# Retention and mixture of experts on one core: tile loads in two halves of 64 partitions, the second one paced by TensorE

## The chip, the core and the metric

The kernel runs on one core of a Trainium2 chip. The metric is the device time of one execution in microseconds, the median of several runs. The profile is that of one further execution. All data are float32; matrix products are done in float32 in the first stage and, in the second, as three products of a high and a low part in a reduced format (a value is split into what the format holds and the rest).

## What is computed

```python
# q, k, v: (8, 8, 576, 64)     retention, causal, with a decay per head
scores = scale * np.matmul(q, k.transpose(0, 1, 3, 2))
ret = scores * Dmat[None, :, :, :]          # Dmat = gamma_h ** (i - j) for j <= i, else 0
attn = np.matmul(ret, v)
x = attn.transpose(0, 2, 1, 3).reshape(4608, 512)

# mixture of 8 experts, top 1
e_idx = np.argmax(x @ w_gate, axis=1)
gate_w = softmax(x @ w_gate)[np.arange(N), e_idx]
eom = 1.0 / (1.0 + np.exp(-(x @ w_output_gate)))
for e in range(8):
    h = np.maximum(x[mask] @ w1[e], 0.0)    # w1: (8, 512, 1024)
    out[mask] = gate_w[mask, None] * eom[mask, e, None] * (h @ w2[e])   # w2: (8, 1024, 512)
```

## The kernel before

There are two stages. The retention stage walks over 36 tiles of 128 tokens (`NTILE`), 9 to two batches, in one loop over `g` (lines 573 to 631). The expert stage then takes the tokens of each expert, at most 616 slots (`CAP`), and multiplies them with the expert's two weight matrices (`mm1`, `mm2`, lines 247 to 290).

A tile's q, k and v lie in DRAM as one block, `pack[g]`: 128 partitions by 3 x 512 numbers, 768 KB. `load(g)` (line 306) takes a buffer from a pool of five (`ld`, `LD = 5`) and issues one DMA on SP's queue. In tile `g` of the loop, `load(g + 4)` is called; the buffer that it gets is the one of tile `g - 1`, whose last reader is `by_state(g - 1)` on TensorE.

The engines keep the order of the program (`manual_schedule`, line 570). In tile `g` that order is, as far as it matters here:

- SP: `load_k(g + 1)` (line 336: for odd tiles from 3 to 31 that don't end a batch pair, k by rows, 256 KB, into one of two buffers that `update` frees), `load(g + 4)`, then by `weights(g)` (line 554) perhaps a block of 512 KB of expert 0's weights. In tile 31 also the first gathered rows and their indices (`load_rows`, `load_idx`), which wait for the scatters issued up to tile 30.
- POOL: `prep(g + 1)` (line 352), which multiplies the tile's v by a decay, giving `vp`; later one or two scatters of finished tokens into the experts' slots (line 629).
- TensorE: `scores(g + 1)` (line 357, q times k, with products on the rows 0 to 63 and 64 to 127 apart), `by_state(g)` (line 399, q times the state), `outT(g)` (line 412: S V, 8 products of the masked scores with `vp`, added to what `by_state` left in PSUM), `update(g)` (line 383, the state), `k_rows(g + 1)` (line 342, k transposed, in the tiles where it isn't loaded), `xnat(g - 1)` (line 525, the finished tile transposed and the gate's logits).
- ACT copies the state (line 396), k and the finished tile out of PSUM; DVE masks the scores (line 378), scales the tile's output (line 422) and works out the gate for four tiles at a time.

Expert 0's weights come in eight blocks in the same loop. `wsched` gives for each the tile of its DMA, of its cast on ACT (`hi_w`) and of its subtraction on DVE (`lo_w`). The table `pe` holds one TensorE instruction; `read(paced=True)` in the expert stage makes a DMA wait for it.

Of the kernel before, what the change touches and what calls it, by code (L numbers as in the profile page):

```python
# [10 lines left out]
F32 = mybir.dt.float32  # L11
# [8 lines left out]
SYNC = mybir.DependencyInfo(mybir.DependencyClass.Sync, mybir.DependencyReason.DATA)  # L20
# [6 lines left out]
P = 128  # L27
NP = H // 2
NTILE = NT // P
# [4 lines left out]
TA = -(-CA // P)  # L34
SNAP = 5
# [5 lines left out]
GT = 4  # L41
# [7 lines left out]
def tile_retention_moe(  # L49
# [16 lines left out]
    V, A, G, T, SP = nc.vector, nc.scalar, nc.gpsimd, nc.tensor, nc.sync  # L66
# [58 lines left out]
    const.tile([P, 16], F32, name="shift0")  # L125
    W1, W2 = {}, {}

    def start_w(which, e, fp):
        src, shape = (w1, [P, KB, 256]) if which == 1 else (w2, [P, 2, DM])
        st = wst.tile(shape, F32, name="st")  # L130
        SP.dma_start(out=st, in_=src[e, fp].rearrange("p (a b) -> p a b", a=shape[1]))
        if which == 2 and not W2:
            wpool.tile([P, 48], F32, name="shift1")
        hi = wpool.tile(shape, F32R, name=f"w{which}h{fp}")
        lo = wpool.tile(shape, F32R, name=f"w{which}l{fp}")
        (W1 if which == 1 else W2)[e, fp] = (hi, lo)
        return st, hi, lo

    def hi_w(st, hi, lo):
        for h in range(2):  # L140
            k = slice(h * st.shape[1] // 2, (h + 1) * st.shape[1] // 2)
            A.copy(out=hi[:, k], in_=st[:, k])  # L142
# [14 lines left out]
    pe = [None]  # L157
# [3 lines left out]
    def read(paced=False, first=None, **kw):  # L161
        i = SP.dma_start(**kw)
        if paced:
            tc.add_manual_dep(i.ins, pe[0].name, SYNC, reason="not before TensorE is at this point")
        for j in scat if first is None else first:
            tc.add_manual_dep(i.ins, j.name, SYNC, reason="reads the rows after every scatter so far")
        tc.add_to_no_dep_group("xs", i.ins)

    def load_rows(e, t, first=None):
        XG[e, t] = xg.tile([P, DM], F32, name="x_g")  # L170
        o, m = e * NT + ROW0[t], ROWS[t]
        read(first=first, out=XG[e, t][0:m], in_=xs[o:o + m, 0:DM])
# [9 lines left out]
    def load_idx(e, part, first=None):  # L182
        ts = range(TA) if part == 0 else range(TA, CT)
        if e == 0 and part == 0:
            for t in ts:
                o, m = ROW0[t], ROWS[t]
                read(first=first, out=idx[0:m, e, t], in_=xs[o:o + m, DM:DM + 2].bitcast(I32))
        else:
            o = e * NT + ROW0[ts[0]]
            read(out=idx[:, e, ts[0]:ts[-1] + 1],  # L190
                 in_=xs[o:o + P * len(ts), DM:DM + 2].rearrange("(t p) w -> p t w", p=P).bitcast(I32))
# [29 lines left out]
    def transp(e, t):  # L221
        transp_lo(*transp_hi(e, t))
# [71 lines left out]
    ld = actx.enter_context(tc.tile_pool(name="ld", bufs=LD, side="right"))  # L294
# [5 lines left out]
    pk, kn, vs, xT, gt = {}, {}, {}, {}, {}  # L300
# [2 lines left out]
    sc = ps_s.tile([P, 2, 512], F32, name="sc")  # L303
    o_ps = ps_s.tile([P, 2, 512], F32, name="o_ps")

    def load(g):
        t = ld.tile([P, 3, 512], F32, name="pk")
        SP.dma_start(out=t, in_=pack[g])
        pk[g] = t

    def load_first():
        t = [ld.tile([P, 3, 512], F32, name="pk") for _ in range(4)]
# [23 lines left out]
    def load_k(g):  # L336

        if g < NTILE and g % CPB != 8 and by_rows(g):
            kn[g] = wk.tile([P, DM], F32, name="kn")
            SP.dma_start(out=kn[g], in_=krow[g])  # L340
# [42 lines left out]
    def update(g):  # L383

        c = g % CPB
        if c == 8:
            return
        if c in (0, 4):
            st_ps[0] = ps_1.tile([P, NP, D], F32, name="st_ps")
        lo = 64 if c == 4 else 0  # L390
        for p in range(NP):
            for r in range(2):
                o = P * p + 64 * r
                T.matmul(st_ps[0][64 * r:64 * r + 64, p, :], lhsT=kn[g][lo:P, o:o + D], rhs=vs[g][lo:P, 2 * p + r, :],  # L394
                         start=(c in (0, 4) and p == 0), stop=True, skip_group_check=True)
        A.copy(out=stT[g % 2], in_=st_ps[0])
        stcur[0] = stT[g % 2]
# [14 lines left out]
    def outT(g, S_sb, state):  # L412
        o = o_ps
        c = g % CPB
        part = lambda p, r: o[64 * ((p + r) % 2):64 * ((p + r) % 2) + 64, r, P * (p // 2):P * (p // 2) + P]

        for r, p in ((r, p) for r in range(2) for p in range(NP)):
            T.matmul(part(p, r), lhsT=vs[g][:, 2 * p + r, :], rhs=S_sb[:, r, p, :],
                     start=(state is None and p < 2), stop=True, skip_group_check=True)
        x = wk.tile([P, NP, P], F32, name="xT")  # L420
        c0 = P * c if c < 5 else 64 + P * (c - 5)
        V.tensor_tensor(out=x.rearrange("p (r s) i -> p r s i", r=2),
                        in0=o[:, :, 0:2 * P].rearrange("p r (s i) -> p r s i", s=2),
                        in1=gq_sb[:, :, c0:c0 + P].rearrange("p (r s) i -> p r s i", r=2), op=ALU.mult)
        xT[g] = x
# [120 lines left out]
    for r in range(2):  # L546
        T.matmul(sc[:, r], lhsT=zx[:, 0:P], rhs=zx[:, 0:512], start=True, stop=True)
    prep(0)

    wsched = {(1, 0): (4, 7, 7), (1, 1): (7, 11, 11), (1, 2): (11, 15, 15), (1, 3): (15, 19, 19),  # L550
              (2, 0): (19, 23, 23), (2, 1): (23, 27, 27), (2, 2): (27, 31, 31), (2, 3): (34, 36, 36)}
    wparts = {}

    def weights(g):
        for w, at in wsched.items():
            if g == at[0]:
                wparts[w] = start_w(w[0], 0, w[1])
            if g == at[1]:
                hi_w(*wparts[w])

    def weights_lo(g, part=range(2)):
        for w, at in wsched.items():
# [7 lines left out]
    with tc.manual_schedule():  # L570
        S_next = scores(0)
        k_rows(0)
        for g in range(NTILE):
            S_sb = S_next
            prev = stcur[0] if g % CPB != 0 else None
            if g < 4:
                load_rest(g)
            load_k(g + 1)
            if g < NTILE - 4:
                load(g + 4)  # L580
            if g == GT * SNAP + 10:
                first = list(scat)
            if g == GT * SNAP + 11:
                for t in range(TA):
                    load_rows(0, t, first)
                load_idx(0, 0, first)
            if g == 0:
                outT(g, S_sb, prev)
            if g + 1 < NTILE:
                prep(g + 1)  # L590
                S_next = scores(g + 1)
            else:
                pools["x_ps"] = lambda: sc[:, 0].rearrange("p (b k i) -> p b k i", b=2, k=2)
                transp(0, 2)
            if prev is not None:
                by_state(g, prev)
            weights(g)
            if g > 0:
                outT(g, S_sb, prev)
            update(g)  # L600
            if "pend" in gt and g % GT == 2:

                gate2(ps_s.tile([P, NP, P], F32, name="k_ps").rearrange("p a i -> p (a i)"))
            if g + 1 < NTILE:
                k_rows(g + 1)

            if "half" in gt:
                gate1b()
            if "fill" in gt:
                gate4()  # L610
            if "ps" in gt:
                gate3a()
            weights_lo(g, (0,))
            weights_lo(g - 1, (1,))
            if g > 0:
                xnat(g - 1)
            if "sl" in gt:
                gate3b()
            if "fill" in gt and g == NTILE - 2:
                gate4()  # L620
            if g % GT == 0 and g > 0:
                gate1a(g // GT - 1)
            if g == NTILE - 1:
                wide = wk.tile([P, H, D], F32, name="vp")
            for _ in range(1 if g < GT * SNAP + 6 else 2 if g < NTILE - 1 else len(todo)):
                if todo:

                    G.memset(gap if g < NTILE - 1 else wide, 0.0)
                    todo.pop(0)()
            if g in (NTILE - 3, NTILE - 2):  # L630
                transp(0, g - NTILE + 3)
# [92 lines left out]
    w = [start_w(1, 1, fp) for fp in range(2)]  # L724
# [58 lines left out]
    with ExitStack() as octx:  # L783
        ov = octx.enter_context(tc.tile_pool(name="ov", bufs=1))
        ps_v = octx.enter_context(tc.tile_pool(name="ps_v", bufs=2, space=PSUM))
        n = nc.values_load(ovn[0:1, 0:1], min_val=0, max_val=NOV)  # L786
        with tc.For_i(0, n, 1) as i:
            e = nc.values_load(ovt[0:1, 0, bass.ds(i, 1)], engines=[mybir.EngineType.SP], min_val=0, max_val=E - 1)
# [5 lines left out]
            for fp in range(4):  # L794
                SP.dma_start(out=wa[:, :, 256 * fp:256 * fp + 256],
                             in_=w1[bass.ds(e, 1), fp].rearrange("a p (k f) -> p (a k) f", k=KB))
            wb = ov.tile([P, FB, DM], F32, name="wb")
            for fp in range(4):
                SP.dma_start(out=wb[:, 2 * fp:2 * fp + 2],
                             in_=w2[bass.ds(e, 1), fp].rearrange("a p (k c) -> p (a k) c", k=2))  # L800
# [6 lines left out]
            for fb in range(FB):  # L807
                h_ps = ps_v.tile([P, P], F32, name="oh_ps")
                for k in range(KB):
                    T.matmul(h_ps, lhsT=wa[:, k, P * fb:P * fb + P], rhs=oxT[:, k, :],  # L810
                             start=(k == 0), stop=(k == KB - 1))
                A.activation(out=oh[:, fb], in_=h_ps, func=AF.Relu)
            y_ps = ps_v.tile([P, DM], F32, name="oy_ps")
            for fb in range(FB):
# [4 lines left out]
                                 in_=y, in_offset=None, bounds_check=NT - 1, oob_is_err=False)  # L819
# [70 lines left out]
```

## Time and profile before

| | |
|---|---|
| median of 3 runs | 605.92 us (605.68 to 607.18) |
| profiled execution | 608.54 us |
| its span, first to last instruction | 606.8 us |
| mean granted TensorE clock | 0.998 |
| HBM read, written | 77.75 MB, 31.18 MB |
| tile loads by `load` | 32, 768 KB each |

Busy times are unions of an engine's instructions. PE is TensorE's multiplying, PEld its loading of the stationary operand; the two overlap. Matmuls are pipelined and their ends are modelled, so a busy PE isn't PE at its peak. An idle stretch is put down to what ended it; "issue" stands where no semaphore explains it.

### The profile page before, as it was taken

Reading aid. Unit: us, or ns where it says so; the run is one execution under the profiler, and the core shown is the slowest. Engines: PE = TensorE matmul, PEld = TensorE weight load, DVE = VectorE, ACT = ScalarE, POOL = GpSimd, SP = SyncE. Lnnn points to the kernel's source line nnn. Section 1 sums busy time; section 2 is a strip of 40 time slices with the busy share of each in tenths; the row PEclk is TensorE's granted clock in tenths of the full one; section 3 lists DMA queues with packets and bytes.
Section 4 is the critical chain, followed back from the end, with each engine's and each line's share of the span. In section 5 each row is a group of like instructions: output and inputs, shape, how many; then the busy total and the mean of one; then the engine's idle time right before and its main releaser. Section 6 shows DMA issues by size and latency. Waiting matters only on the chain. (4 is left out here: it accounts for less than half of the span.)

```text
span 606.8 us, 13985 instructions
## 1 busy us (share of the span) xinstructions
PE 591.9 (98%) x5688; PEld 529.0 (87%) x5688; DVE 332.2 (55%) x731; ACT 220.4 (36%) x481; POOL 188.2 (31%) x235
## 2 busy tenths in 40 slices
PE   8999999999999999999999999999999999999995
PEld 6789888878898999879978987997899799889974
DVE  3599898888660666625543554445265435625410
ACT  2334333323331544324433443433354344325110
POOL 2245544575456624016013301601250110110011
PEclk9999999999999999999999999999999999999999
DMA  9979889985226676434343634444263334221011
GB/s 314 373 284 328 327 293 313 343 277 195 91 89 194 173 196 195 136 122 136 109 138 116 175 104 136 116 138 139 96 188 92 119 104 143 103 83 52 1 38 42
DMA packets 56925, 100.28 MB, mean 165 GB/s; under 512 B 14839, under 2 KB 35832, under 8 KB 56860
## 3 DMA queue, kind: packets, MB, share of 16 engines
q1 hardware_dynamic: 46988, 76.72, 39.7%
q0 software_dynamic: 9440, 21.60, 9.8%
q8 instruction: 45, 0.74, 0.5%
q10 hardware_dynamic: 432, 1.05, 0.5%
q14 instruction: 20, 0.16, 0.1%
HBM read 77.75 MB, written 31.18 MB: 180 GB/s over the span
## 5 line engine op out<-in xcount | busy, mean ns | idle before, releaser
L262 PE MATMUL h_ps<-xh,w1h 128*128 128x360 f32 (+1 forms) x512 | 155.3, 303 | 0.1
L262 PE MATMUL h_ps<-xh,w1l 128*128 128x360 f32 (+1 forms) x512 | 155.0, 303 | 0.0
L262 PE MATMUL h_ps<-xl,w1h 128*128 128x360 f32 (+1 forms) x512 | 154.9, 303 | 0.0
L289 POOL DMA_INDIRECT out_dram<-y,idx x40 | 40.2, 1005 | 314.1 <-ACT y L288 264.3
L270 DVE SCALAR_TENSOR_TENSOR hl<-h_ps,hh 128x360 fp32r<-128x360 f32 (+1 forms) x128 | 61.2, 478 | 129.3 <-ACT hh L269 115.8
L283 PE MATMUL y_ps<-w2h,hh 128*128 128x512 f32 (+1 forms) x320 | 124.9, 390 | 0.0
L283 PE MATMUL y_ps<-w2l,hh 128*128 128x512 f32 (+1 forms) x320 | 124.9, 390 | 0.0
L283 PE MATMUL y_ps<-w2h,hl 128*128 128x512 f32 (+1 forms) x320 | 124.6, 389 | 0.0
L269 ACT ACTIVATE hh<-h_ps 128x360 fp32r<-128x360 f32 (+1 forms) x128 | 54.9, 429 | 118.1 <-PE h_ps L262 112.1
L262 PEld LDWEIGHTS h_ps<-xh,w1h 128*128 128x128 f32 x512 | 96.0, 188 | 0.6 <-DVE xl L245 0.3
L262 PEld LDWEIGHTS h_ps<-xl,w1h 128*128 128x128 f32 x512 | 96.3, 188 | 0.3
L262 PEld LDWEIGHTS h_ps<-xh,w1l 128*128 128x128 f32 x512 | 96.0, 188 | 0.0
L288 ACT ACTIVATE y<-y_ps,idx 128x512 f32<-128x512 f32 (+1 forms) x40 | 27.5, 689 | 138.7 <-issue 90.1
L147 DVE TENSOR_TENSOR w1l<-st,w1h 128x512 fp32r<-128x512 f32 x64 | 46.0, 755 | 48.1 <-ACT w1h L142 46.7
L283 PEld LDWEIGHTS y_ps<-w2h,hl 128*128 128x128 f32 (+1 forms) x320 | 58.8, 184 | 14.1
L283 PEld LDWEIGHTS y_ps<-w2h,hh 128*128 128x128 f32 (+1 forms) x320 | 58.8, 184 | 13.8
L283 PEld LDWEIGHTS y_ps<-w2l,hh 128*128 128x128 f32 (+1 forms) x320 | 58.8, 184 | 13.6
L194 POOL DMA_INDIRECT xs<-xgrp,sli x36 | 39.0, 1083 | 62.5 <-issue 34.5
L194 POOL DMA_INDIRECT xs<-zx,fill x42 | 45.5, 1083 | 7.1 <-issue 6.4
L354 POOL TENSOR_TENSOR vp<-pk,con_sb 128x512 f32<-128x512 f32 x36 | 37.8, 1052 | 29.6 <-PE st_ps L394 12.9
L378 DVE TENSOR_TENSOR S_sb<-sc,con_sb 128x512 f32<-128x512 f32 x64 | 41.0, 682 | 10.2 <-PE sc L367 9.1
L147 DVE TENSOR_TENSOR w2l<-st,w2h 128x512 fp32r<-128x512 f32 x64 | 44.6, 735 | 2.3
(128 smaller groups left out, 672.2 us busy)
## 6 DMA issues: line engine op xcount, KB each, us to landing
st<-in_w_dram SPq DMA_DIRECT2D x64, 512.0 KB
pk<-in_pack_dram SPq DMA_DIRECT2D x32, 768.0 KB
x_q<-xs SPq DMA_DIRECT2D x140, 64.0 KB
kn<-in_krow_dram SPq DMA_DIRECT2D x14, 256.0 KB
gq_sb<-in_gq_dram SPq DMA_DIRECT2D x5, 256.0 KB
pk<-in_pack_dram SPq DMA_DIRECT2D x4, 256.0 KB
pk<-in_pack_dram SPq DMA_DIRECT2D x2, 512.0 KB
x_g<-xs SPq DMA_DIRECT2D x4, 256.0 KB
```

The lines of the kernel that those rows point to most:

```text
L147: V.tensor_tensor(out=lo[:, k], in0=st[:, k], in1=hi[:, k].bitcast(F32), op=ALU.subtract)
L194: i = G.indirect_dma_start(out=xs, out_offset=bass.IndirectOffsetOnAxis(ap=at, axis=0), in_=x, in_offset=None, **({} if bound is None else ...
L262: i = T.matmul(ps, lhsT=a[:, k, :], rhs=b[:, k, 0:n], start=(j == 0), stop=(j == 3 * KB - 1))
L269: A.activation(out=hh, in_=ps, func=AF.Relu)
L270: V.scalar_tensor_tensor(out=hl, in0=ps, scalar=0.0, in1=hh.bitcast(F32), op0=ALU.max, op1=ALU.subtract)
L283: i = T.matmul(ps, lhsT=a[:, n], rhs=b, start=(j == 0), stop=(j == 3 * FB - 1))
L288: A.activation(out=y, in_=ps, func=AF.Copy, scale=idx.bitcast(F32)[0:m, e, t, 1:2])
L289: G.indirect_dma_start(out=out, out_offset=bass.IndirectOffsetOnAxis(ap=idx[0:m, e, t, 0:1], axis=0), in_=y, in_offset=None, bounds_check= ...
L354: G.tensor_tensor(out=vs[g], in0=pk[g][:, 2].rearrange("p (h d) -> p h d", h=H), in1=gk_sb[:, g % CPB].broadcast_to([P, H, D]), op=ALU.mult)
L378: V.tensor_tensor(out=v(S_sb[:, r].rearrange("p a i -> p (a i)")), in0=v(sc[:, r]), in1=cmat_sb[:, 0:2].rearrange("p c a i -> p a (c i)"). ...
```

## The change

`load` is split. The first call, at the old place, takes the buffer and loads partitions 0 to 63; the second, behind `update(g)` in the program, loads partitions 64 to 127 and gets a manual dependency on the instruction in `pe`, which `outT` now sets to the last S V product of the tile. A block of expert 0's weights is loaded in two halves of its free dimension, in two different tiles (2 tiles apart, but for the last block). The gathered rows of tile 31 are issued behind `update`, after the last half load.

```diff
-    def start_w(which, e, fp):
+    def load_st(st, src, i, n):
+        k = slice(i * st.shape[1] // n, (i + 1) * st.shape[1] // n)
+        SP.dma_start(out=st[:, k], in_=src.rearrange("p (a b) -> p a b", a=st.shape[1])[:, k])
+
+    def start_w(which, e, fp, part=range(1)):
...
-        SP.dma_start(out=st, in_=src[e, fp].rearrange("p (a b) -> p a b", a=shape[1]))
+        for i in part:
+            load_st(st, src[e, fp], i, len(part))
...
-    def load(g):
-        t = ld.tile([P, 3, 512], F32, name="pk")
-        SP.dma_start(out=t, in_=pack[g])
-        pk[g] = t
+    def load(g, half):
+
+        if half == 0:
+            pk[g] = ld.tile([P, 3, 512], F32, name="pk")
+        n = slice(64 * half, 64 * half + 64)
+        i = SP.dma_start(out=pk[g][n], in_=pack[g, n])
+        if half == 1:
+            tc.add_manual_dep(i.ins, pe[0].name, SYNC, reason="not before TensorE is at this point")
...
-            T.matmul(part(p, r), lhsT=vs[g][:, 2 * p + r, :], rhs=S_sb[:, r, p, :],
-                     start=(state is None and p < 2), stop=True, skip_group_check=True)
+            i = T.matmul(part(p, r), lhsT=vs[g][:, 2 * p + r, :], rhs=S_sb[:, r, p, :],
+                         start=(state is None and p < 2), stop=True, skip_group_check=True)
+        pe[0] = i.ins
...
-    wsched = {(1, 0): (4, 7, 7), (1, 1): (7, 11, 11), (1, 2): (11, 15, 15), (1, 3): (15, 19, 19),
-              (2, 0): (19, 23, 23), (2, 1): (23, 27, 27), (2, 2): (27, 31, 31), (2, 3): (34, 36, 36)}
+
+    wsched = {(1 + i // 4, i % 4): (3 + 4 * i, 5 + 4 * i, 7 + 4 * i) for i in range(7)}
+    wsched[2, 3] = (33, 34, 36)
...
-        for w, at in wsched.items():
+        for (which, fp), at in wsched.items():
             if g == at[0]:
-                wparts[w] = start_w(w[0], 0, w[1])
+                st, hi, lo = wparts[which, fp] = start_w(which, 0, fp, ())
+                load_st(st, (w1, w2)[which - 1][0, fp], 0, 2)
             if g == at[1]:
-                hi_w(*wparts[w])
+                load_st(wparts[which, fp][0], (w1, w2)[which - 1][0, fp], 1, 2)
+            if g == at[2]:
+                hi_w(*wparts[which, fp])
...
             if g < NTILE - 4:
-                load(g + 4)
+                load(g + 4, 0)
             if g == GT * SNAP + 10:
                 first = list(scat)
-            if g == GT * SNAP + 11:
-                for t in range(TA):
-                    load_rows(0, t, first)
-                load_idx(0, 0, first)
...
             update(g)
+            if g < NTILE - 4:
+                load(g + 4, 1)
+            if g == GT * SNAP + 11:
+                for t in range(TA):
+                    load_rows(0, t, first)
+                load_idx(0, 0, first)
```

## The prediction, made before the result was known

> **What bounds the kernel now.** I read the page first, then the busy time by stretches, then the order of time on TensorE and on SP's queue, and last the waits. The columns of the stretches are start:end, length, busy time of PE, PEld, DVE, ACT and POOL with counts, granted clock, DMA share, GB/s.
>
> ```profile
> span 606.8 us, 13985 instructions
> ...
> PE 591.9 (98%) x5688; PEld 529.0 (87%) x5688; DVE 332.2 (55%) x731; ACT 220.4 (36%) x481; POOL 188.2 (31%) x235
> ```
> ```profile
> 0.00:162.00 162.00, 154.45 (x3169) 134.74 (x3169) 127.83 (x362) 57.75 (x157) 74.96 (x109) 1.00 0.82 288
> 162.00:590.00 428.00, 427.74 (x2479) 386.54 (x2479) 204.34 (x370) 161.28 (x323) 110.38 (x125) 1.00 0.40 124
> ```
> ```profile
> 0.00:15.00 15.00, 12.82 (x197) 9.11 (x198) 5.75 (x9) 4.32 (x10) 4.16 (x11) 1.00 0.93 313
> ```
>
> TensorE sets the time. In the expert stage, 162 to 590 us, it is idle for 0.26 us, and the change touches nothing there. All that it touches runs in the first 162 us, the retention stage, where TensorE is idle for 162.00 − 154.45 = 7.55 us. Of that, 2.18 us lie in the first 15 us, while the first tiles are fetched. So 5.4 us of idle time are left that a smoother supply could give back: that is the most that this change can gain by filling gaps, and a gain by anything else would need shorter matmuls, which it doesn't make.
>
> The two longest of these gaps stand in the middle of the S V products (L418):
>
> ```profile
> 20.49 0.88 PE L418 MATMUL o_ps<-S_sb,vp 128*64 128x128 f32 x12
> 22.44 0.44 PE L418 MATMUL o_ps<-S_sb,vp 128*64 128x128 f32 x4 [1.08 <-issue]
> ```
> ```profile
> 86.72 0.88 PE L418 MATMUL o_ps<-S_sb,vp 128*64 128x128 f32 x12
> 88.84 0.44 PE L418 MATMUL o_ps<-S_sb,vp 128*64 128x128 f32 x4 [1.25 <-issue]
> ```
> ```profile
> ## 3 DMA queue, kind: packets, MB, share of 16 engines
> ...
> q8 instruction: 45, 0.74, 0.5%
> ```
> ```profile
> 21.00:22.00 1.00, 0.36 (x8) 0.12 (x4) 0.49 (x1) 0.00 (x0) 0.00 (x0) 1.00 1.06 407
> 84.00:87.00 3.00, 3.00 (x75) 2.62 (x72) 2.79 (x11) 2.15 (x5) 0.00 (x0) 1.00 1.00 412
> 88.00:89.00 1.00, 0.15 (x2) 0.16 (x4) 1.00 (x3) 0.00 (x0) 0.45 (x1) 1.00 0.18 72
> ```
>
> "Issue" means that no semaphore explains the wait, and both waits stop after 12 of 16 identical products, where the operands had long been used by the products before. What is left is the supply of instructions: 45 transfers of 0.74 MB in all, some 16 KB each, on the same 16 DMA engines. Both gaps fall in or right behind a stretch in which those engines are full (407 and 412 GB/s). That the full queue delays the instructions is my inference; the trace shows only the coincidence.
>
> **The supply is bursty.** SP's queue and the stretches show why:
>
> ```profile
> 24.02 0.38 SPq L308 DMA_DIRECT2D pk<-in_pack_dram  x1
> 24.45 0.42 SPq L131 DMA_DIRECT2D st<-in_w_dram  x1
> 26.29 0.33 SPq L308 DMA_DIRECT2D pk<-in_pack_dram  x1
> 31.80 0.33 SPq L340 DMA_DIRECT2D kn<-in_krow_dram  x1
> 32.18 2.84 SPq L308 DMA_DIRECT2D pk<-in_pack_dram  x2
> ```
> ```profile
> 26.00:30.00 4.00, 4.00 (x102) 3.55 (x92) 2.58 (x8) 1.12 (x3) 1.04 (x1) 1.00 1.01 398
> 30.00:33.00 3.00, 3.00 (x55) 2.76 (x48) 2.99 (x6) 0.94 (x3) 1.07 (x2) 1.00 0.47 154
> ```
> ```profile
> st<-in_w_dram SPq DMA_DIRECT2D x64, 512.0 KB
> pk<-in_pack_dram SPq DMA_DIRECT2D x32, 768.0 KB
> ```
>
> Two tile loads of 768 KB leave close together, a weight block of 512 KB between, at 398 GB/s; then the rate falls to 154. The pattern repeats every two tiles.
>
> **The held half.** load(g+4) now leaves when its buffer is free, after by_state(g−1). After the change its first 64 partitions keep that wait, and the other 64 wait until S V of tile g is done. Tile 9 (g = 5) shows the lead that is given away:
>
> ```profile
> 25.77 0.41 PE L409 MATMUL o_ps<-pk,stT 64*64 64x64 f32 x16
> 28.93 0.90 PE L367 MATMUL sc<-pk 64*64 64x128 f32 x32
> 30.20 1.09 PE L418 MATMUL o_ps<-S_sb,vp 128*64 128x128 f32 x16
> 31.12 0.63 PE L394 MATMUL st_ps<-vp,kn 128*64 128x64 f32 x16
> 37.28 0.90 PE L367 MATMUL sc<-pk 64*64 64x128 f32 x32
> 41.22 0.90 PE L367 MATMUL sc<-pk 64*64 64x128 f32 x32
> ```
>
> The load is issued at 26.29 and scores(9) read it at 41.22: 14.9 us. The held half will leave at about 31.3 (30.20 + 1.09), so 9.9 us remain. At 398 GB/s a half (393 KB) takes 1.0 us and everything that can stand ahead of it, a half, a krow block and half a weight block, under 2.5 us. I put the lost lead at nothing; TensorE's own work covers it, and if the cover were gone (rates halved, below) each late microsecond would be one of TensorE's.
>
> Behind the waiting SP instruction are queued load_k(g+2), the first half of load(g+5), and the next weight half. load_k(g+2) already waits for update(g), which follows S V directly (31.12 behind 30.20), so it loses nothing; the next tile's first half moves from by_state to the end of S V, about 1 us of its 15. SP issues 32 tile halves and 8 weight halves more, 0.33 to 0.42 us each by the rows above, some 15 us of SP's time in a stage where it mostly waits: nothing on the path. Per pair of tiles the same bytes leave in four lots, two behind each S V, instead of one.
>
> **Weights.** The casts stay at tiles 7, 11 and so on. The second half now leaves at tile 5 + 4i, two tiles (37.28 − 28.93 = 8.35 us) ahead of its cast; nothing on the path by the same rates. If it came late, ACT would wait in its cast with the state copy (L396) behind it, and by_state on TensorE after that.
>
> **The gathered rows** (three x_g and three idx loads) move behind the last half of tile 35's load.
>
> ```profile
> SPq L162 <- DMA xs<-xgrp,sli: 10.5, 1, 10.5
> ```
> ```profile
> 139.44 1.09 PE L418 MATMUL o_ps<-S_sb,vp 128*64 128x128 f32 x16
> ```
> ```profile
> 146.84 1.32 SPq L162 DMA_DIRECT2D x_g<-xs  x3
> 148.21 1.40 SPq L162 DMA_DIRECT2D idx<-xs  x3
> ```
>
> They wait for scatters until 146.84, and S V of tile 31 ends at 140.5, so they leave when they do now. The one weight block behind them has until tile 36. Nothing.
>
> **New waits.** A reader of all 128 partitions, the product on POOL (L354), now waits for two transfers, and scores has one wait per half. Where a wait needs an instruction of its own, its price is
>
> ```profile
> L418 PEldq EVENT_SEMAPHORE  x4: 51/51/51, 7.6 to 120.2; - x4
> ```
>
> Between nothing and 32 × 0.051 = 1.6 us if every one stood on TensorE. Only four such instructions occur on S V in 36 tiles, so I stay near the lower end: 0.4 us.
>
> **The sum.** The two gaps give back 1.08 + 1.25 = 2.33 us, if thinner bursts keep the instructions supplied; the bounds are 0 and the 5.4 us of all idle time. Less 0.4, the change is −1.9 us: the profiled execution took 608.54 us (its span 606.8 and 1.7 around it) and would take 606.6. The median of the runs, 605.92, lies 2.6 below the profiled execution; the same difference gives 604.0.
>
> On these gaps the Trainium skill has a rule, in "Runtime: NRT & Kernel Launch", section "Instruction fetch mechanics": instructions are refilled in 16 KiB blocks and the crossing of a block is mostly hidden. The size agrees with 0.74 MB in 45 transfers; the 1.08 and 1.25 us here don't look hidden. By that rule the two gaps are something else and the sum is the 605.9 of the second case below.
>
> **Rival: a half goes at half the rate, and DMA becomes the bound (slower).** A transfer to 64 partitions may reach fewer paths into the memory than one to 128. The trace doesn't say: its loads are to 128, except
>
> ```profile
> L162 SPq DMA_DIRECT2D x_q<-xs x140: 311/430/1266, 194.3 to 500.9; - x140
> ```
>
> which go to 32 partitions, but with 64 KB per 0.43 us of issuing (152 GB/s) they ask for too little to meet a limit of half of 398. If it holds, four halves per pair of tiles take 1.573 MB / 199 = 7.9 us, and krow and weights, 0.524 MB at 398, another 1.3: 9.2 us against the 8.35 us in which TensorE does two tiles. Missing are 0.87 us per pair, 14 us over 16 pairs; the lead of some 6 us that is left when two halves queue has to be used up first, at tile 4 + 2 × 7 or so, and from there TensorE waits for each tile. That gives +8 us, 614; the ends are +1, if scattering and loading share better than I think and the halves overlap, and +14 and more, if the scattered rows add to it. For it speaks the arithmetic, which needs only the rate; against it, that no row shows the limit.
>
> The Trainium skill states the limit, in "SBUF — State Buffer", section "Door 1: The DMA port swizzle (why `[64,N]` ≈ `[32,N]`)": partitions 0 to 63 reach 8 of 16 ports, 196 GB/s against 328 at 1 MiB, and two such transfers don't run side by side. No run here shows it yet; by its 196 the sum is that of this rival.
>
> **Rival: nothing moves.** The bursts were hidden anyway and the gaps have another cause, or come back at other places. For it: after 15 us there is one wait for a tile's load on POOL,
>
> ```profile
> POOL vp L354 <- DMA pk<-in_pack_dram: 1.9, 1, 1.9
> ```
>
> and the rest of the idle time, from 124 to 146 us, follows POOL's scatters and products, which the change leaves alone. 605.9, give or take 0.9.
>
> That the change doesn't spread the loads at all is excluded by its wait: S V ends some 5 us after by_state of the tile before.
>
> **How the numbers follow.** A measurement of this kernel can tell about 0.3%, 1.8 us, from no change. Forecast, gaps filled: chance 0.43, 604.0, own range 602.5 to 606.0; it lies across the bound, so 0.34 faster, 0.08 same, 0.01 slower. Half rate: 0.39, 614, from 606.9 to 622; 0.37 slower, 0.02 same. Nothing moves: 0.18, 605.9; 0.16 same, 0.02 faster. Together 0.36 faster, 0.26 same, 0.38 slower: the likeliest single case is a small gain, although a loss is as likely as a gain. The range 602.5 to 615 holds nearly all of the first and third case and a little over half of the second, about 0.8.
>
> **What would show it.** Right: the two gaps behind 12 of 16 S V products gone or under 0.5 us, idle time of TensorE up to 162 us at 5 to 6 us instead of 7.55, no stretch at 398 followed by one at 154, no wait of POOL or TensorE for pk after 15 us. Half rate: the stretches of the first 150 us stay near or below 300 GB/s at a DMA share of 1, POOL's product and scores wait for pk in tile after tile from about 80 us on, and the expert stage begins some 8 us later at unchanged length. Nothing moves: gaps of over 1 us marked "issue" at other tiles. The forecast is wrong if the retention stage doesn't end earlier, or if the expert stage changes length.

## The result, and the profile after

| | before | changed |
|---|---|---|
| median | 606.55 us (605.56 to 608.27, 6 runs) | 638.22 us (634.97 to 641.87, 6 runs) |
| ratio | | 1.0508, interval 1.0483 to 1.0533 |
| profiled execution, its span | 608.54, 606.8 us | 638.13, 636.3 us |

The change makes the kernel 5% slower. The page of the changed kernel, the line of the engines, then the granted clock, the DMA share and the rate in 40 slices of 15.9 us:

```profile
PE 603.2 (95%) x5688; PEld 537.7 (85%) x5688; DVE 335.1 (53%) x731; ACT 222.1 (35%) x481; POOL 187.6 (29%) x235
...
PEclk8998988998899999999999999999999999999999
DMA  9999999999932576634434354353444425231001
GB/s 294 222 216 269 253 263 249 277 269 249 264 111 87 200 197 182 198 103 143 137 101 134 129 149 143 97 165 104 135 128 135 132 80 166 84 112 50 1 33 43
```

DMA is full in the first eleven slices, and yet the rate there is lower than before. In the stretch from 15 to 135 us, with a DMA share of 1.03 (the view can read a little above 1), the changed kernel moves 248 GB/s:

```profile
15.00:135.00 120.00, 103.77 (x2070) 91.55 (x2063) 81.96 (x224) 37.24 (x99) 46.04 (x62) 0.94 1.03 248
```

The kernel before has 317 GB/s there, at a share of 0.89 (its row stands further down, with the run of every other tile). Full engines that move less: that is the first thing to see. The stretches of the changed kernel, cut where the first product of the expert stage begins, and then those of before, cut at the same place:

```profile
0.00:191.80 191.80, 165.94 (x3170) 143.52 (x3170) 131.06 (x363) 59.66 (x158) 74.72 (x109) 0.94 0.96 244
191.80:619.60 427.80, 427.62 (x2478) 386.54 (x2479) 204.04 (x369) 161.08 (x322) 110.02 (x125) 1.00 0.40 123
```
```profile
0.00:162.20 162.20, 154.57 (x3170) 134.75 (x3170) 128.03 (x363) 57.91 (x157) 75.16 (x109) 1.00 0.82 288
162.20:590.00 427.80, 427.62 (x2478) 386.53 (x2479) 204.14 (x369) 161.11 (x322) 110.18 (x125) 1.00 0.40 123
```

The expert stage is 427.80 us long in both. All of the loss, 191.8 − 162.2 = 29.6 us, lies in the retention stage. TensorE does the same 3170 records there; it is idle for 25.9 us instead of 7.6, which is 18.2 us more, and it is busy for 11.4 us more, at a granted clock of 0.94 instead of 1.00.

What TensorE waits for, from 15 us to the end of the stage (changed kernel, then the S V products of before; total, times, longest):

```profile
PEld o_ps L427 <- issue: 14.5, 30, 2.9
...
PE o_ps L427 <- issue: 9.3, 4, 2.8
...
PE st_ps L403 <- DMA kn<-in_krow_dram: 7.4, 8, 1.7
...
POOL vp L363 <- DMA pk<-in_pack_dram: 7.2, 1, 7.2
...
PEld st_ps L403 <- issue: 5.2, 7, 1.9
```
```profile
PE o_ps L418 <- issue: 2.3, 2, 1.3
```

Not for the halves themselves. It waits in the state products (L403) for krow's block, which stands in the same queue, and most of all for nothing that a semaphore explains: in the S V products alone 9.3 us in four waits, instead of 2.3 us in two. The two largest of these, on TensorE:

```profile
23.15 0.88 PE L427 MATMUL o_ps<-S_sb,vp 128*64 128x128 f32 x12
26.53 0.44 PE L427 MATMUL o_ps<-S_sb,vp 128*64 128x128 f32 x4 [2.51 <-issue]
28.55 0.71 PE L403 MATMUL st_ps<-vp,kn 128*64 128x64 f32 x16 [1.58 <-DMA kn<-in_krow_dram]
```
```profile
104.38 0.88 PE L427 MATMUL o_ps<-S_sb,vp 128*64 128x128 f32 x12
108.01 0.70 PE L427 MATMUL o_ps<-S_sb,vp 128*64 128x128 f32 x4 [2.76 <-issue]
```

These are the two gaps of before, behind the same 12 of 16 records. They have not gone; 1.08 has become 2.51 and 1.25 has become 2.76. The other two, of 2.17 and 1.86 us, stand in tiles that had no such gap before. Around the first of the four the clock can be seen to fall (the third number from the end, before the DMA share):

```profile
23.70:26.50 2.80, 0.32 (x6) 0.08 (x2) 0.45 (x1) 0.00 (x0) 0.00 (x0) 1.00 1.17 239
26.50:30.00 3.50, 1.89 (x24) 1.56 (x25) 0.69 (x1) 0.37 (x1) 0.60 (x1) 0.87 1.02 219
30.00:34.00 4.00, 4.00 (x70) 3.65 (x70) 1.08 (x4) 1.33 (x3) 0.44 (x1) 0.69 1.02 207
31.00:32.00 1.00, 1.00 (x6) 0.87 (x4) 0.17 (x1) 0.37 (x1) 0.00 (x0) 0.50 1.19 268
34.00:38.00 4.00, 4.00 (x91) 3.44 (x88) 2.62 (x9) 1.12 (x3) 1.04 (x1) 1.00 1.07 226
```

TensorE falls idle at 24.0 (23.15 + 0.88), waits 2.51 us and soon after 1.58 us more. In the four microseconds from 30 the clock is 0.69 on average, and TensorE, busy all the time, does 70 records instead of the 91 of the four after (partly other products). In steps of one microsecond from 29 to 33 it is 0.54, 0.50, 0.50 and 0.75, and then 1.00 again. So a gap can cost twice: its own length, and a slow stretch behind it. Seven such stretches, each some 3.4 us at 0.50, lie in the retention stage of the changed kernel, all close behind one or two waits that add up to 1.6 us or more; together 12.0 us of full clock are missing, which fits the 11.4 us of longer busy time. The kernel before has no such stretch in this stage.

### The profile page after: what moved, and what is told of

Read it like the earlier page. It is cut to its first block, busy times and chain, and to the rows that moved or that the text cites. A ratio compares the mean times of both kernels' runs of the same rounds, so it can differ in the third digit from the quotient of the medians.

```text
span 636.3 us, 14058 instructions
## 1 busy us (share of the span) xinstructions
PE 603.2 (95%) x5688; PEld 537.7 (85%) x5688; DVE 335.1 (53%) x731; ACT 222.1 (35%) x481; POOL 187.6 (29%) x235
## 5 line engine op out<-in xcount | busy, mean ns | idle before, releaser
L293 ACT ACTIVATE y<-y_ps,idx 128x512 f32<-128x512 f32 (+1 forms) x40 | 27.5, 688 | 138.8 <-issue 90.1
L152 DVE TENSOR_TENSOR w1l<-st,w1h 128x512 fp32r<-128x512 f32 x64 | 48.6, 796 | 48.1 <-ACT w1h L147 46.8
L427 PE MATMUL o_ps<-S_sb,vp 128*64 128x128 f32 x576 | 42.4, 288 | 9.3 <-issue 9.3
```

What stands on the lines that cost most here:

```text
L152: V.tensor_tensor(out=lo[:, k], in0=st[:, k], in1=hi[:, k].bitcast(F32), op=ALU.subtract)
L293: A.activation(out=y, in_=ps, func=AF.Copy, scale=idx.bitcast(F32)[0:m, e, t, 1:2])
L427: i = T.matmul(part(p, r), lhsT=vs[g][:, 2 * p + r, :], rhs=S_sb[:, r, p, :], start=(state is None and p < 2), stop=True, skip_group_check ...
```

## The experiments

Theory 1 was now that a transfer that writes 64 partitions moves at about half the rate, so that the retention stage becomes bound by DMA. Its rivals: theory 2, the hold, which lets everything behind it on SP come late; theory 3, more and smaller transfers, whatever they write.

**Halves of 64 partitions without the hold** (on the kernel before):

```diff
-        SP.dma_start(out=t, in_=pack[g])
+        for n in (slice(0, 64), slice(64, P)):
+            SP.dma_start(out=t[n], in_=pack[g, n])
```

> The kernel before, with each tile's 768 KB load as two DMAs of 64 partitions one right behind the other at the old place; nothing is held, the weights come as before. Theory 1 (a transfer that writes 64 partitions moves at half the rate): still slower by 25 to 35 us, 630 to 642, with 200 to 270 GB/s at a DMA share of 1 in the retention stage. Theory 2 (the hold: what is queued on SP behind the waiting half comes late): 605 to 608, as before. Theory 3 (more and smaller transfers cost more, whatever they write): also slower, 630 to 642.

633.18 us (632.13 to 634.53), ratio 1.0443 (1.0415 to 1.0471). The hold isn't needed for the loss: these two lines alone bring 26.5 us. The stage shows the same picture:

```profile
0.00:186.00 186.00, 161.63 (x3169) 141.39 (x3169) 127.15 (x363) 59.20 (x157) 75.19 (x109) 0.95 0.95 251
```

**Halves by columns, held** (on the changed kernel):

```diff
-        n = slice(64 * half, 64 * half + 64)
-        i = SP.dma_start(out=pk[g][n], in_=pack[g, n])
+        n = slice(768 * half, 768 * half + 768)
+        i = SP.dma_start(out=pk[g].rearrange("p a b -> p (a b)")[:, n],
+                         in_=pack[g].rearrange("p a b -> p (a b)")[:, n])
```

> The changed kernel, but a tile's block is halved along its 1536 columns: each half writes all 128 partitions (3 KB each); second half held as in the change, weights in halves. Theory 1 (64 partitions, half the rate): the loss is gone, 603 to 608. Theory 2 (the hold): 635 to 641, as changed. Theory 3 (smaller transfers): 630 to 641.

606.63 us (605.41 to 607.27), ratio 0.9996 (0.9983 to 1.0009). As many transfers of the same size, with the same hold and the same weight halves, and no loss. Theory 3 falls, and theory 2 as a cause of its own. This kernel also tests what the prediction hoped for, since it is the change with the full rate. Its stretches, and the gap in tile 3:

```profile
26.00:30.00 4.00, 4.00 (x104) 3.55 (x98) 2.36 (x7) 1.12 (x3) 1.04 (x1) 1.00 0.97 354
30.00:33.00 3.00, 3.00 (x63) 2.76 (x56) 2.96 (x7) 0.66 (x2) 0.82 (x1) 1.00 0.71 250
```
```profile
22.71 0.44 PE L428 MATMUL o_ps<-S_sb,vp 128*64 128x128 f32 x4 [1.14 <-issue]
...
117.41 0.44 PE L428 MATMUL o_ps<-S_sb,vp 128*64 128x128 f32 x4 [1.31 <-issue]
```

The supply is indeed evener, 354 and 250 GB/s instead of 398 and 154. It gains nothing: the gap of tile 3 is 1.14 us instead of 1.08, and one of 1.31 us stands in a later tile.

**The weight halves alone** (the changed kernel with `load` whole again, at the old place and without the hold):

```diff
         if half == 0:
             pk[g] = ld.tile([P, 3, 512], F32, name="pk")
-        n = slice(64 * half, 64 * half + 64)
-        i = SP.dma_start(out=pk[g][n], in_=pack[g, n])
-        if half == 1:
-            tc.add_manual_dep(i.ins, pe[0].name, SYNC, reason="not before TensorE is at this point")
+            SP.dma_start(out=pk[g], in_=pack[g])
```

> Of the change only the weight halves and the later place of the gathered rows; a tile's block is loaded whole at the old place, without a hold. Theories 1 and 2: 605 to 608, as before, since weight halves write 128 partitions and nothing holds them. Theory 3 (smaller transfers): slower by 3 us or more, since 8 blocks are split.

607.17 us (606.06 to 609.77), ratio 1.0004 (0.9982 to 1.0026): nothing, and nothing from the later place of the gathered rows either.

**The loads by themselves:**

```python
    def whole(j):
        SP.dma_start(out=t[j], in_=src[j])

    def parts(j, n, other=None):
        for k in range(0, P, n):
            (other if other and k else SP).dma_start(out=t[j][k:k + n], in_=src[j][k:k + n])
    ...
    def rows64(j):
        for k in range(2):
            SP.dma_start(out=t[j][:, 768 * k:768 * k + 768],
                         in_=src[j][64 * k:64 * k + 64].rearrange("p (c b) -> (p c) b", c=2))
    ...
    stages = [whole, partial(parts, n=64), columns, rows64, partial(parts, n=64, other=A), pairs, whole]
```

> Only loads: 20 tile blocks of 768 KB (15.7 MB) into 20 buffers, seven times, with all of a round landed before the next begins; retention and experts are left out, and the output is filled with loaded numbers. Rounds: whole; two partition halves of 64; two column halves; 64 rows of the source spread over 128 partitions; partition halves on SP's and ACT's queue; quarters of 32 partitions in the order 0, 64, 32, 96; whole again. Theory 1: whole 38 to 42 us (near 400 GB/s), partition halves 70 to 80, columns and spread rows 38 to 44, two queues and quarters still over 60. Theory 2: all rounds alike, 38 to 44. Theory 3: columns and spread rows as slow as the partition halves, quarters slower than these.

This kernel only loads and computes nothing; it ran once. One stretch from the middle of each round, in the order of the rounds (the columns: start:end, length, busy DVE, busy POOL, clock, DMA share, GB/s):

```profile
5.00:35.00 30.00, 0.00 (x0) 0.00 (x0) 1.00 1.02 420
52.00:118.00 66.00, 0.77 (x7) 0.00 (x0) 1.00 0.98 222
126.00:160.00 34.00, 0.00 (x0) 0.00 (x0) 1.00 1.03 397
174.00:208.00 34.00, 0.00 (x0) 0.00 (x0) 1.00 1.02 394
222.00:276.00 54.00, 0.00 (x0) 0.00 (x0) 1.00 1.02 262
290.00:340.00 50.00, 0.00 (x0) 0.00 (x0) 1.00 1.02 286
352.00:385.00 33.00, 0.00 (x0) 0.00 (x0) 1.00 1.01 418
```

Whole 420 GB/s, halves of 64 partitions 222, and the engines are busy all the time in both. Halving by columns costs 5% (397). The same 64 rows of DRAM, spread over 128 destination partitions, go at 394: it is the place written to that counts, not which rows of DRAM are read. Two queues bring 262, quarters that alternate between the two sides of partition 64 bring 286: transfers to different sides overlap a little.

The Trainium skill, "SBUF — State Buffer", section "Door 1: The DMA port swizzle (why `[64,N]` ≈ `[32,N]`)", gives this as ports: partitions 0 to 63 reach 8 of 16. The trace agrees on the size, 222 of 420 is 0.53. Where the same page of the Trainium skill, in its section "Can I just issue two DMAs to hit both halves?", has only 6% more for two concurrent transfers to both halves than for one, the 262 and 286 here differ: 18 and 29%.

**The hold alone:** the changed kernel with the block whole, in one DMA, held until S V.

```diff
-        if half == 0:
+        if half == 1:
             pk[g] = ld.tile([P, 3, 512], F32, name="pk")
-        n = slice(64 * half, 64 * half + 64)
-        i = SP.dma_start(out=pk[g][n], in_=pack[g, n])
-        if half == 1:
+            i = SP.dma_start(out=pk[g], in_=pack[g])
             tc.add_manual_dep(i.ins, pe[0].name, SYNC, reason="not before TensorE is at this point")
```

> The changed kernel, but a tile's block is loaded whole, in one DMA, and the whole of it is held until S V of tile g is done (weights in halves). Half rate as the only cause: 605 to 608, since 9.9 us of lead are left and nothing is slow. The hold as a cause of its own, which would explain the 5 us between the changed kernel (638) and the halves without hold (633): 609 to 613.

607.75 us (605.74 to 610.39), ratio 1.0008 (0.9984 to 1.0031). At the full rate the hold costs nothing that can be measured.

**Every other tile in halves:**

```diff
-        SP.dma_start(out=t, in_=pack[g])
+        for n in (slice(0, 64), slice(64, P)) if g % 2 == 0 else (slice(0, P),):
+            SP.dma_start(out=t[n], in_=pack[g, n])
```

> The kernel before, with the load in two DMAs of 64 partitions for the even tiles alone, no hold. Capacity (the DMA engines have room until they are full): before, they are busy for 0.81 of 147 us, so 28 us are free; a split load takes 786 KB / 230 GB/s - 786 KB / 420 GB/s = 1.55 us more, 16 of them 25 us: they fit, 606 to 611. Each split load delays TensorE by itself: half of 26.5 us, 617 to 623.

622.45 us (619.09 to 625.66), ratio 1.0261 (1.0202 to 1.0321). My expectation from capacity was wrong: half of the splits didn't fit, they cost a little over half. The fault is in the room that I assumed. I had spread the free time over the whole stage, and a good part of it lies behind the last load, where it is of no use. The stretch in which loads run, in the kernel before and then here:

```profile
15.00:135.00 120.00, 116.21 (x2486) 102.98 (x2487) 99.71 (x282) 42.88 (x119) 60.08 (x83) 1.00 0.89 317
```
```profile
15.00:135.00 120.00, 110.74 (x2305) 98.55 (x2302) 92.87 (x260) 41.82 (x113) 50.81 (x69) 0.97 1.00 287
```

At a share of 0.89, 13 us of 120 are free, not 28. With 16 × 1.55 = 25 us more work the engines are full, and 12 us are missing; measured were 15.4. That half the splits bring about half the loss would also follow if each split delayed TensorE by itself, so this run doesn't tell these two apart; the ballast run below shows what full engines do without any split.

**Quarters across partition 64:**

```diff
-        SP.dma_start(out=t, in_=pack[g])
+        for k in (0, 64, 32, 96):
+            SP.dma_start(out=t[k:k + 32], in_=pack[g, k:k + 32])
```

> The kernel before, with each load in four DMAs of 32 partitions, first partitions 0, then 64, 32 and 96 (288 GB/s alone), no hold. Capacity: a load takes 2.73 us instead of 1.87, 32 of them 27.5 us more against 28 free: at the edge, 606 to 614. If the number of transfers were what counts: four per tile, so at least the 633 of two per tile.

619.2 us (617.54 to 620.83), ratio 1.0199 (1.0152 to 1.0247). Twice as many transfers as in the halves, and less than half the loss: the rate counts, not the number. The 606 to 614 that I expected rested on the same 28 us of room, and missed. With 13 us of room the sum is 27.5 − 13 = 14.5 us, and 12.1 were measured.

**Ballast** (the kernel before, loads whole):

```diff
         SP.dma_start(out=t, in_=pack[g])
+        SP.dma_start(out=ballast[g], in_=pack[g].rearrange("p a b -> p (a b)")[:, 0:1280])
```

> The kernel before, loads whole, and behind each of them one more DMA of 655 KB from the same block into unused DRAM, over all 16 DMA engines: 1.56 us at 420 GB/s per tile, what a split costs. Capacity: full DMA engines alone bring the loss, 625 to 640, with the same waits (for krow's block and marked issue, and a clock below 1 behind them). If the loss needs writes to 64 partitions: 605 to 610.

630.36 us (629.62 to 631.7), ratio 1.0377 (1.0328 to 1.0426). No write to 64 partitions is in it, and TensorE loses 23.3 us. Its stretch, and its waits from 15 us on:

```profile
15.00:135.00 120.00, 103.67 (x2111) 91.75 (x2111) 83.82 (x234) 37.43 (x100) 47.52 (x64) 0.94 1.02 404
```
```profile
PE st_ps L396 <- DMA kn<-in_krow_dram: 16.4, 9, 4.8
...
PEld st_ps L396 <- issue: 5.6, 4, 5.0
PEld o_ps L420 <- issue: 5.5, 27, 0.5
```

So full DMA engines are enough for a loss of this kind, with the same clock of 0.94. The parts differ: here krow's block is most of it. The gaps marked "issue" in the S V products stay at 0.5 us or less, although the share is 1.02; with the halves they are the larger part. Long gaps of that sort seem to need the slow transfers, not full engines alone.

The sum that fitted the two runs above to within 4 us is too high here: 32 × 1.56 − 13 = 37 us against 23.3. It is too high for the halves without hold as well, 50 − 13 = 37 against 26.5. One part of this is that a split cost less in place than I took: with these halves the stage has 0.95 × 186.1 = 177 us of DMA work instead of 133, so 44 more and not 50. What makes the rest stays open.

**What "issue" is:** the halves without hold, and four small products of zeros ahead of the first tile, which are 8 records more on PE.

```diff
         T.matmul(sc[:, r], lhsT=zx[:, 0:P], rhs=zx[:, 0:512], start=True, stop=True)
+        for _ in range(2):
+            T.matmul(sc[:, r, 0:64], lhsT=zx[:, 0:P], rhs=zx[:, 0:64], start=True, stop=True)
```

> The halves without hold, with four small products of zeros (8 records on PE) added ahead of the first tile. In every kernel so far a gap marked issue stands behind the 12th of the 16 records of S V of tile 3, wherever DMA is. If it is TensorE waiting for its next block of instructions, the gap moves with the count of instructions: it stands behind the 4th of the 16 here. If it is a wait of that product for something, it stays behind the 12th.

629.91 us in one run. TensorE in tile 3:

```profile
22.73 0.44 PE L419 MATMUL o_ps<-S_sb,vp 128*64 128x128 f32 x4
26.67 0.91 PE L419 MATMUL o_ps<-S_sb,vp 128*64 128x128 f32 x12 [3.49 <-issue]
```

The gap has moved ahead by exactly the 8 records. (The expectation's "every kernel so far" is too wide: with the quarters the 16 records of tile 3 show no gap.) The count of records from the start to the gap shows it too, and not for this gap alone. First here, then in the kernel before up to its two gaps, then in the changed kernel up to the same two (each stretch ends just before the product behind the gap; the counts are the numbers behind x, on PE and PEld):

```profile
0.00:26.62 26.62, 21.44 (x348) 16.92 (x348) 9.72 (x18) 6.34 (x15) 5.62 (x12) 1.00 0.98 264
```
```profile
0.00:22.39 22.39, 19.18 (x348) 14.53 (x348) 9.72 (x18) 6.34 (x15) 5.63 (x12) 1.00 0.98 330
0.00:88.79 88.79, 84.12 (x1739) 72.37 (x1739) 66.04 (x181) 31.70 (x84) 36.06 (x53) 1.00 0.92 324
```
```profile
0.00:26.48 26.48, 20.07 (x348) 15.16 (x348) 9.71 (x18) 6.34 (x15) 5.62 (x12) 0.94 1.00 266
0.00:107.96 107.96, 90.72 (x1739) 77.50 (x1740) 67.03 (x181) 32.33 (x84) 37.16 (x54) 0.94 1.02 254
```

The gaps of over 0.6 us marked "issue" in the retention stages of these three, of the halves without hold and of the columns all stand at such places, 348 on PE or a whole number of steps of 126.5 behind it. A step is 253 records of PE and PEld together, and the whole list, 2 × 5688 records in the 45 instruction transfers of the profile, makes 253 for each transfer. So a gap belongs to a place in the list of instructions, not to a product or its operands: TensorE waits for its next block of instructions. That its transfer is late because it shares the DMA engines with the loads is likely (the profile counts the 45 transfers on the same 16 engines), but wasn't tested by itself.

The Trainium skill, "Runtime: NRT & Kernel Launch", section "Instruction fetch mechanics", which the prediction cites, calls such a crossing mostly hidden. With halves of 64 partitions under way the one in tile 3 is 2.5 to 3.5 us here; with ballast it is 0.26 us.

**Halves and hold, weights whole:** the changed kernel with the old `wsched` and whole weight blocks.

```diff
-    wsched = {(1 + i // 4, i % 4): (3 + 4 * i, 5 + 4 * i, 7 + 4 * i) for i in range(7)}
-    wsched[2, 3] = (33, 34, 36)
+    wsched = {(1, 0): (4, 7, 7), (1, 1): (7, 11, 11), (1, 2): (11, 15, 15), (1, 3): (15, 19, 19),
+              (2, 0): (19, 23, 23), (2, 1): (23, 27, 27), (2, 2): (27, 31, 31), (2, 3): (34, 36, 36)}
...
-                st, hi, lo = wparts[which, fp] = start_w(which, 0, fp, ())
-                load_st(st, (w1, w2)[which - 1][0, fp], 0, 2)
+                wparts[which, fp] = start_w(which, 0, fp)
```

> The changed kernel, but expert 0's weights are loaded whole at their old tiles: 64-partition halves, the second held, the rows later. If the hold adds the 5 us between 633 (halves without hold) and 638 (the change) once DMA is full: 636 to 640. If the weight halves add them: 631 to 635.

636.06 us (632.89 to 639.97), ratio 1.0481 (1.0425 to 1.0537). The value lies between the halves without hold (1.0443) and the change (1.0508), and its interval overlaps both. Between those two lie 5 us by the medians and 4 us by the ratios; their intervals just don't touch (up to 1.0471, from 1.0483), so some difference is likely, and which part of the change makes it stays open. After 15 us TensorE waited eight times for krow's block in the changed kernel (7.4 us) and once, for 3.6 us, with the halves alone, which points to the hold and proves nothing.

## Why the prediction was wrong

**The step that failed** is the price of the held half: "I put the lost lead at nothing". It took the rate of 128 partitions, 398 GB/s, for a transfer to 64, the held half and the other alike, and these move at 222. At 222 a tile's load takes 786 KB / 222 = 3.5 us of all DMA engines, and at 420 it takes 1.9. The rival that said this had a chance of 0.39; the forecast went to the case that the rows of before could show, and they could not show this one, because nothing in that kernel writes 64 partitions at full demand.

**The rival's size was wrong as well**, +8 us against 31.7. Two terms. It left the scattered rows out of the sum, and so believed that 8.35 us per pair of tiles faced only 9.2; the share of 0.89 says directly that 13 us of 120 were free. Against that stand 32 loads with some 1.55 us more each, 50 us (1.55 is for 230 GB/s, as in the expectation above). The whole stage bears it out: DMA's busy time was 0.82 × 162.2 = 133 us and is 0.96 × 191.8 = 184 us, 51 more, and the stage is now hardly longer than DMA's work in it. The difference of the two, 37 us, is more than the 29.6 by which the stage grew, so this sum explains the size only roughly. And the rival counted TensorE's waits at their length alone; the longer busy time at the lower clock behind them is 11.4 of the 29.6 us.

**The rival's path was wrong too.** It expected scores and POOL's product to wait for the halves tile after tile. After 15 us POOL's product waited for them once, for 7.2 us, and TensorE not at all. The tile loads have the longest lead: 9.9 us are left for the held half. krow's block has less: in the kernel before it is issued at 23.60 and read at 31.12, 7.5 us later, and in the changed kernel the one issued at 21.97 is what TensorE waits for until 28.55. No row shows the lead of an instruction block. krow's block and the instructions were late first.

**The gaps.** That they are the supply of instructions was right, as the shifted gap shows. That a thinner supply would close them was wrong: with columns the bursts are thinner, the gap of tile 3 is 1.14 us, and another of 1.31 stands elsewhere. The 2.33 us of the forecast were never there to be had in this way.

**What held:** the expert stage didn't change; weight halves and the later rows cost nothing; the hold by itself costs nothing at full rate (607.75, and the lead of 9.9 us covers it as worked out); extra waits cost too little to be seen (the columns have them too, at a ratio of 0.9996).

## What to carry to other kernels

Halve a transfer along its free dimension, not along its partitions: the same bytes in as many transfers went at 397 GB/s by columns and at 222 by partitions. Before making any transfer slower, read the DMA share in the stretch where the transfers run, not over the stage, and take (1 − share) × length as the room. That sum came within 4 us where the extra work was 25 to 28 us, and was 7 to 14 us too high where it was 50: it says whether the room is used up, and the size only roughly. When DMA fills up, look first at a small block that is loaded late and at the instructions themselves, rather than at the buffers that are deep.

## What the runs showed of the hardware

- Loads from DRAM that write 64 partitions each: 222 GB/s against 420 for 128, in one run; which rows of DRAM are read doesn't matter (394 for 64 rows spread over 128 partitions). The DMA share doesn't show it, it is 0.98 and 1.02; rate and share have to be read together.
- Transfers to the two sides of partition 64 overlap in part: 262 GB/s from two queues, 286 in alternating quarters from one.
- A gap on TensorE without a semaphore can be its instructions. It kept its place in the count of instructions when products were added ahead of it, is 1.1 us in tile 3 before and 2.5 to 3.5 us there with every load in halves of 64 partitions. With ballast, where the engines are as full but no transfer writes 64 partitions alone, none of these in S V was over 0.5 us; why a full engine alone doesn't lengthen them was not tested further.
- After waits of TensorE within a busy stage the granted clock fell to 0.50 for some 3.4 us: in the changed kernel after 2.51 and 1.58 us, and after a single one of 1.66 us (0.50 at 81 us). After the gaps of 1.08 and 1.25 us of the kernel before it stayed at 1.00, but it also stayed there after a wait of 2.79 us, at 73 us, in the run with four more products. The length of a wait alone doesn't decide it; what does wasn't tested.
